# Rounding casts of the weight pieces queued behind the exponentials in a fused attention and feed-forward kernel

## Chip, cores, metric

The kernel runs on one core of one Trainium2 chip. The metric is the device time of one execution in microseconds; the time before is the median of three runs.

## What is computed

Block-causal attention (8 batches, 8 heads, 576 positions, 64 columns a head), whose output goes through two matrix products with a piecewise quadratic between them. Cut to what matters:

```python
scores = scale * np.matmul(q, k.transpose(0, 1, 3, 2))
scores = np.where(block_i >= block_j, scores, -1000000000.0)     # blocks of 64
attn = np.exp(scores - max) / (sum + 1e-09)
x = np.matmul(attn, v)                                           # -> 4608 x 512
h = x @ w_in                                                     # 512 x 2048
g = np.where(h >= 1, h, np.where(h <= -1, 0, (h + 1) ** 2 / 4))
out = g @ w_out                                                  # 2048 x 512
```

## The kernel before

TensorE multiplies in float32r, and float32 operands are split into a rounded part (hi) and the rest (lo). Three streams of work share the engines.

**Attention.** `attention_steps` goes through 32 pairs of heads (a batch and two neighbouring heads), eight steps a pair. A step traces one group of scores: `scores` (two products a tile on TensorE at L482 and L485, the row maximum on VectorE at L505, the exponential on ScalarE at L509, the inverse of the sum at L491 and L492, and the scaling of the probabilities `pr` on VectorE at L515), or `scores_last` (L529 to L541). Some steps later the probabilities are transposed (`turn`, L552 or L554), copied out of PSUM (L545) and multiplied with v (`weighted`, L591); the result is copied to `xh` and `xl` (L626, L627). The queries and keys of the next pair are prepared on the way: loads at L334 and L339, splits at L351 to L364, transposes at L422, copies at L427 and a copy by DMA at L433. The pairs of the first two batches are the eight that share their time with the weights. From the second batch on the probabilities are first moved by a DMA at L243.

**Weights.** `weight_pieces` cuts both matrices into 64 pieces of 128 x 256; `convert` splits one, in three stages that `prepare_weights` advances: (1) the load into `bits` (L164), two scalings on ScalarE (L169, L170), three operations on VectorE (L171, L174, L177); (2) an integer add on GpSimd (L183) and the rounding cast on ScalarE (L185) to `wih` or `ws`; (3) the subtract on GpSimd (L187), which leaves the lo part and lets the buffers go. The second piece of each pair of w_out pieces also stores the split rows to DRAM (L213). The feed-forward work reads them back (L787). `bits` and `work` have three buffers each, and odd pieces below 32 borrow the feed-forward buffers `t` and `gl`.

**Feed-forward.** `ffn_in` (L770 to L787) and `ffn_out` (L794 to L811) work on 512 tokens and 128 hidden columns a tile.

What sets the order: the main loop traces one step of attention, then the conversion stages that are due, then (from step 36) one half of a feed-forward tile. A scheduler then puts the traced instructions into one fixed order for each engine, and may take an instruction that is ready early ahead of others that were traced before it. At run time each engine and the SP queue, which issues all DMAs, take their instructions in that order, and wait with semaphores. So a cast at L185 may stand ahead of the exponentials of the step in which it was traced, or of earlier ones.

Of the kernel before, what the change touches and what calls it, by code (L numbers as in the profile page):

```python
# [23 lines left out]
def block_attn_then_ffn(  # L24
# [9 lines left out]
    nc = tc.nc  # L34
# [116 lines left out]
    for j in range(2):  # L151
        nc.sync.dma_start(qa[D:KA, j, :S].bitcast(F32), mrow[:, 0, :].bitcast(F32))
        nc.sync.dma_start(ka[D:KA, j, :].bitcast(F32), mrow[:, 1, :].bitcast(F32))


    def convert(n, source, hi, lo, done):

        if n < BORROW and n % 2:
            bits = ffn.tile([P, CW, 2], I32, tag="t", name="bits")
            work = ffn.tile([P, 2, CW], F32, tag="gl", name="work")  # L160
        else:
            bits = conv.tile([P, CW, 2], I32, tag="bits", name="bits")
            work = conv2.tile([P, 2, CW], F32, tag="work", name="work")
        nc.sync.dma_start(bits, source.bitcast(I32).rearrange("p (n t) -> p n t", t=2))  # L164
        top, mag = work[:, 0, :], work[:, 1, :].bitcast(U32)
        low = bits[:, :, 0]


        nc.scalar.mul(top, bits[:, :, 1].bitcast(F32), 2.0**-112)  # L169
        nc.scalar.mul(low, low.bitcast(U32), 2.0**-29)  # L170
        nc.vector.tensor_scalar(  # L171
            out=top, in0=top, scalar1=F32_TOP, scalar2=-F32_TOP, op0=ALU.min, op1=ALU.max
        )
        nc.vector.tensor_scalar(  # L174
            out=mag, in0=top.bitcast(U32), scalar1=3, scalar2=None, op0=ALU.logical_shift_left
        )
        nc.vector.scalar_tensor_tensor(  # L177
            out=mag, in0=top.bitcast(U32), scalar=0x80000000, in1=mag,
            op0=ALU.bitwise_and, op1=ALU.bitwise_or,
        )  # L180
        yield
        w32 = mag.bitcast(I32)
        nc.gpsimd.tensor_tensor(out=w32, in0=w32, in1=low, op=ALU.add)  # L183
        w32 = w32.bitcast(F32)
        nc.scalar.copy(hi(), w32)  # L185
        yield
        nc.gpsimd.tensor_tensor(out=lo(), in0=w32, in1=hi().bitcast(F32), op=ALU.subtract)  # L187
        if done:
            done()
# [65 lines left out]
    class Pair:  # L255
# [238 lines left out]
        def scores(self, j, g):  # L494
            tiles = self.GROUPS[g]
            m = len(tiles)
            ps = work_bank("ps_s")
            pr = att3.tile([P, S], F32, tag="pr", name="pr")
            nm = small.tile([P, 2], F32, tag="nm", name="nm")
            sm = small.tile([P, 2], F32, tag="sm", name="sm")  # L500
            cols = [slice(at, at + (t + 1) * P) for t, at in tiles]
            for (t, _), cs in zip(tiles, cols):
                self.product(ps[:, cs], j, t * P, 0, (t + 1) * P, True, True)
            for i, cs in enumerate(cols):
                nc.vector.tensor_reduce(  # L505
                    out=nm[:, i : i + 1], in_=ps[:, cs], axis=AX.X, op=ALU.max, negate=True
                )
            for i, cs in enumerate(cols):
                nc.scalar.activation(  # L509
                    pr[:, cs], ps[:, cs], AF.Exp, bias=nm[:, i : i + 1], scale=1.0,  # L510
                    accum_out=sm[:, i : i + 1],
                )
            self.inverse(sm[:, :m])
            for i, cs in enumerate(cols):
                nc.vector.tensor_scalar_mul(pr[:, cs], pr[:, cs], sm[:, i : i + 1])  # L515
            self.pr[j, g] = as_float32r(pr[:, : cols[-1].stop], self.plain) if self.hop else [pr]

        def scores_last(self):

            half = S // 2  # L520
            pr = att3.tile([P, S], F32, tag="pr", name="pr")
            nm = small.tile([P, 3], F32, tag="nm", name="nm")
            sm = small.tile([P, 3], F32, tag="sm", name="sm")
            banks = []
            for i in range(2):
                ps = work_bank("ps_s")
                for j in range(2):
                    self.product(ps[:, :half], j, SM, i * half, half, j == 0, j == 1)
                nc.vector.tensor_reduce(  # L529
                    out=nm[:, i : i + 1], in_=ps[:, :half], axis=AX.X, op=ALU.max, negate=True  # L530
                )
                banks.append(ps)
            nc.vector.tensor_tensor(out=nm[:, 2:3], in0=nm[:, 0:1], in1=nm[:, 1:2], op=ALU.min)
            for i in range(2):
                nc.scalar.activation(
                    pr[:, i * half : (i + 1) * half], banks[i][:, :half], AF.Exp,
                    bias=nm[:, 2:3], scale=1.0, accum_out=sm[:, i : i + 1],
                )
            nc.vector.tensor_tensor(out=sm[:, 2:3], in0=sm[:, 0:1], in1=sm[:, 1:2], op=ALU.add)
            self.inverse(sm[:, 2:3])  # L540
            nc.vector.tensor_scalar_mul(pr, pr, sm[:, 2:3])  # L541
            self.pr["last"] = as_float32r(pr, self.plain) if self.hop else [pr]
# [342 lines left out]
```

## Time and profile before

| | |
|---|---|
| median of 3 runs | 1266.43 us (1266.29 to 1266.98) |
| the profiled execution | 1269.69 us, of which 1267.9 us are the span that the profile shows |
| TensorE (PE) busy | 1200.1 us, 95% of the span |
| VectorE (DVE) busy | 887.0 us, 70% |
| ScalarE (ACT) busy | 703.2 us, 55% |
| GpSimd (POOL) busy | 394.6 us, 31% |
| casts at L185 | 64, at 13.5 to 253.1 us |

The span is the time from the first to the last instruction; the shares are averages over it, and the kernel has stages with different limits: the weights are converted only up to about 255 us. A row of a timeline gives the start, the duration, the engine, the line, what is written from what, and in brackets the idle time of the engine just before it and what ended that.

### The profile page before, as it was taken

The page shows a single profiled execution, that of the slowest core. Times are in us where ns is not written, and L with a number is a line of the kernel's source. Part 1 is how long each engine was busy: PE and PEld are TensorE (multiplying, and loading weights), DVE is VectorE, ACT ScalarE, POOL GpSimd, SP SyncE. Part 2 cuts the span into 40 slices and gives each one's busy share as a digit, 9 for nine tenths or more (in the row PEclk, how much of TensorE's full clock was granted, in tenths as well). Part 3 has the DMA queues.
Part 4 walks back from the last instruction along what each step waited for, and adds up shares of the span by engine and source line. Part 5 has one row for each costly group of instructions (what it writes and reads, how often), then busy time and mean ns, then how long its engine had stood idle before and what let it go on. Part 6 is the DMA issues. An engine that isn't in the chain of part 4 may idle for free.

```text
span 1267.9 us, 20253 instructions
## 1 busy us (share of the span) xinstructions
PE 1200.1 (95%) x6280; PEld 998.8 (79%) x6280; DVE 887.0 (70%) x2188; ACT 703.2 (55%) x1827; POOL 394.6 (31%) x430
## 2 busy tenths in 40 slices
PE   5888889899999999999999999999999999999998
PEld 4666667678888888888888888888888888888886
DVE  8898877758777777777777777787777777322222
ACT  5787656646566655665656655566556555222222
POOL 3555655522222222222222222222222222222222
PEclk9888988999999999999999999999999999999999
DMA  5566666667888655555554655465556433422432
GB/s 158 167 176 215 203 228 197 217 198 237 260 273 266 215 162 158 154 175 163 156 162 145 187 157 152 138 189 153 160 154 190 137 128 118 132 87 98 133 100 100
DMA packets 185259, 215.43 MB, mean 170 GB/s; under 512 B 113840, under 2 KB 132272, under 8 KB 184384
## 3 DMA queue, kind: packets, MB, share of 16 engines
q1 hardware_dynamic: 185152, 214.14, 54.9%
q8 instruction: 50, 0.82, 0.3%
q14 instruction: 57, 0.47, 0.1%
HBM read 134.74 MB, written 31.98 MB: 131 GB/s over the span
## 4 chain that ended last, share of the span: by engine, by line
PE 69%; DVE 16%; ACT 6%; issue 5%; DMA 1%; POOL 1%; SPq 1%; ACTq 0%; POOLq 0%; DVEq 0%
PE ph L770 29%; PE po L794 15%; PE po L799 7%; PE ps_av L591 7%; PE ps_s L482 4%; ACT pr L509 3%; PE ps_s L485 3%; DVE t L780 2%; PE ps_t L552 2%; DVE t L783 2%; ACT t L779 2%; DVE pb L547 2%; DVE nm L505 2%; DVE sm L491 1%; DVE pr L515 1%
## 5 line engine op out<-in xcount | busy, mean ns | idle before, releaser
L785 POOL TENSOR_TENSOR gl<-t,gh 128x512 fp32r<-128x512 f32 x144 | 187.5, 1302 | 510.2 <-ACT gh L784 333.2
L794 PE MATMUL po<-wo,gh 128*128 128x512 f32 x1152 | 296.1, 397 | 0.5 <-DMA wo<-wo_split 0.3
L794 PEld LDWEIGHTS po<-wo,gh 128*128 128x128 f32 x1152 | 212.5, 189 | 44.5 <-DMA wo<-wo_split 0.7
L770 PE MATMUL ph<-xh,wih 128*128 128x512 f32 x576 | 232.9, 404 | 1.6 <-DVE t L783 1.6
L770 PE MATMUL ph<-xh,wil 128*128 128x512 f32 x576 | 228.8, 397 | 0.0
L770 PE MATMUL ph<-xl,wih 128*128 128x512 f32 x576 | 227.8, 396 | 0.5 <-DVE xl L627 0.5
L780 DVE SCALAR_TENSOR_TENSOR t<-t 128x512 f32<-128x512 f32 x144 | 101.5, 705 | 168.0 <-ACT t L779 165.2
L779 ACT ACTIVATE t<-ph 128x512 f32<-128x512 f32 x144 | 85.9, 597 | 173.8 <-PE ph L770 173.8
L509 ACT ACTIVATE pr<-ps_s,nm 128x128 f32<-128x128 f32 (+3 forms) x256 | 134.1, 527 | 60.5 <-DVE nm L505 58.4
L784 ACT CAST gh<-t 128x512 fp32r<-128x512 f32 x144 | 89.5, 621 | 120.3 <-DVE t L783 120.0
L799 PE MATMUL po<-wo,gl 128*128 128x512 f32 x576 | 155.6, 392 | 0.0
L482 PE MATMUL ps_s<-ka,qa 68*128 68x288 f32 (+4 forms) x384 | 135.3, 367 | 15.0 <-ACT pr L509 5.4
L379 POOL TENSOR_TENSOR vsr<-vn,vsr 128x256 fp32r<-128x256 f32 (+1 forms) x96 | 55.2, 576 | 246.2 <-ACT vsr L378 244.6
L770 PEld LDWEIGHTS ph<-xh,wil 128*128 128x128 f32 x576 | 109.5, 190 | 23.8
L770 PEld LDWEIGHTS ph<-xh,wih 128*128 128x128 f32 x576 | 109.8, 191 | 21.7 <-DVE t L783 2.3
L799 PEld LDWEIGHTS po<-wo,gl 128*128 128x128 f32 x576 | 108.7, 189 | 23.1
L505 DVE TENSOR_REDUCE nm<-ps_s 128x1 f32<-128x128 f32 (+3 forms) x256 | 118.8, 482 | 10.4 <-PE ps_s L485 9.4
L770 PEld LDWEIGHTS ph<-xl,wih 128*128 128x128 f32 x576 | 109.7, 190 | 20.5 <-DVE xl L627 0.9
L485 PE MATMUL ps_s<-kb,qb 128*128 128x288 f32 (+4 forms) x384 | 121.1, 322 | 0.0
L515 DVE TENSOR_SCALAR pr<-pr,sm 128x128 f32<-128x128 f32 (+3 forms) x256 | 107.3, 440 | 5.4
L783 DVE TENSOR_TENSOR t<-ph,t 128x512 f32<-128x512 f32 x144 | 98.7, 686 | 2.2
L491 DVE TENSOR_SCALAR sm<-sm 128x1 f32<-128x1 f32 (+1 forms) x224 | 52.0, 232 | 68.3 <-ACT pr L509 65.7
(111 smaller groups left out, 1871.4 us busy)
## 6 DMA issues: line engine op xcount, KB each, us to landing
wo<-wo_split SPq DMA_DIRECT2D x144, 512.0 KB, 3.5
prr<-pr SPq DMA_DIRECT2D x96, 192.0 KB, 2.5
prr<-pr SPq DMA_DIRECT2D x72, 256.0 KB, 2.8
out_dram<-ob SPq DMA_DIRECT2D x36, 256.0 KB, 2.9
bits<-in_moe_w_in_dram SPq DMA_DIRECT2D x32, 256.0 KB, 3.5
bits<-in_moe_w_out_dram SPq DMA_DIRECT2D x32, 256.0 KB, 3.0
wo_split<-ws SPq DMA_DIRECT2D x16, 512.0 KB, 2.9
qa<-qb SPq DMA_DIRECT2D x63, 128.0 KB, 2.4
```

What stands on the lines that cost most here:

```text
L482: nc.tensor.matmul(ps, qa[:KA, j, c0 : c0 + P], ka[:KA, j, k0 : k0 + n], start=first, stop=False)
L485: nc.tensor.matmul(ps, qb[:, j, c0 : c0 + P], kb[:, j, k0 : k0 + n], start=False, stop=last)
L505: nc.vector.tensor_reduce(out=nm[:, i : i + 1], in_=ps[:, cs], axis=AX.X, op=ALU.max, negate=True)
L509: nc.scalar.activation(pr[:, cs], ps[:, cs], AF.Exp, bias=nm[:, i : i + 1], scale=1.0, accum_out=sm[:, i : i + 1],)
L515: nc.vector.tensor_scalar_mul(pr[:, cs], pr[:, cs], sm[:, i : i + 1])
L770: nc.tensor.matmul(ph, w[:, cc, fs], x[:, cc, xs], start=(cc == 0 and i == 0), stop=(cc == NCC - 1 and i == 2),)
L779: nc.scalar.activation(t_, ph, AF.Relu, bias=0.5, scale=0.5)
L780: nc.vector.scalar_tensor_tensor(out=t_, in0=t_, scalar=1.0, in1=t_, op0=ALU.min, op1=ALU.mult)
L783: nc.vector.tensor_tensor(out=t_, in0=ph, in1=t_, op=ALU.max)
L785: nc.gpsimd.tensor_tensor(out=gl, in0=t_, in1=gh.bitcast(F32), op=ALU.subtract)
L794: nc.tensor.matmul(po[tt], gh[:, ts_], wo[:, w, :], start=(fc == 0 and w == 0), stop=False)
L799: nc.tensor.matmul(po[tt], gl[:, ts_], wo[:, 0, :], start=False, stop=fc == NFC - 1)
```

## The change

The exponentials are collected in a list as they are traced, and the rounding cast gets an ordering edge to the latest of them: on ScalarE it is issued behind that exponential. The edge sets the order in the queue and adds no wait of its own. No instruction is added or removed.

```diff
+    exps = []
+
...
         w32 = w32.bitcast(F32)
-        nc.scalar.copy(hi(), w32)
+
+        with tc.issue_after(exps[-1].ins):
+            nc.scalar.copy(hi(), w32)
         yield
...
             for i, cs in enumerate(cols):
-                nc.scalar.activation(
+                exps.append(nc.scalar.activation(
                     pr[:, cs], ps[:, cs], AF.Exp, bias=nm[:, i : i + 1], scale=1.0,
                     accum_out=sm[:, i : i + 1],
-                )
+                ))
...
             for i in range(2):
-                nc.scalar.activation(
+                exps.append(nc.scalar.activation(
                     pr[:, i * half : (i + 1) * half], banks[i][:, :half], AF.Exp,
                     bias=nm[:, 2:3], scale=1.0, accum_out=sm[:, i : i + 1],
-                )
+                ))
```

In the rows of order below the lines of the changed kernel stand two higher inside `convert` ahead of the cast (L171 is L173, L174 is L176, L177 is L179, L164 is L166) and four higher from the cast on (L185 is L189, L491 is L495, L505 is L509, L509 is L513, L515 is L519, L213 is L217, L433 is L437).

ScalarE, the first pair: the first cast and the exponentials of the first step, before.

```order
L169 ACTIVATE work<-bits 128x256
L185 CAST wih<-work 128x256
L456 CAST kb<-ps_qk 128x2x64
L170 ACTIVATE bits<-bits 128x256
L509 ACTIVATE pr,sm<-ps_s,nm 128x128
L509 ACTIVATE pr,sm<-ps_s,nm 128x256
L509 ACTIVATE pr,sm<-ps_s,nm 128x384
```

The same place now.

```order
L171 ACTIVATE work<-bits 128x256
L172 ACTIVATE bits<-bits 128x256
L460 CAST kb<-ps_qk 128x2x64
L513 ACTIVATE pr,sm<-ps_s,nm 128x128
L513 ACTIVATE pr,sm<-ps_s,nm 128x256
L189 CAST wih<-work 128x256
L513 ACTIVATE pr,sm<-ps_s,nm 128x384
```

The cast went behind two exponentials. Of the 64 casts 30 have more exponentials ahead of them than before, 29 as many and 5 fewer, since the scheduler places everything anew.

VectorE, the second half of the fourth pair, from the scaling of the last rows' probabilities on, before (twelve consecutive rows).

```order
L515 TENSOR_SCALAR pr<-pr,sm 128x256
L491 TENSOR_SCALAR sm<-sm 128x1
L177 SCALAR_TENSOR_TENSOR work<-work 128x256
L492 RECIPROCAL sm<-sm 128x1
L174 TENSOR_SCALAR work<-work 128x256
L515 TENSOR_SCALAR pr<-pr,sm 128x384
L505 TENSOR_REDUCE nm<-ps_s 128x1
L177 SCALAR_TENSOR_TENSOR work<-work 128x256
L171 TENSOR_SCALAR work<-work 128x256
L174 TENSOR_SCALAR work<-work 128x256
L177 SCALAR_TENSOR_TENSOR work<-work 128x256
L491 TENSOR_SCALAR sm<-sm 128x1
```

The same place now.

```order
L519 TENSOR_SCALAR pr<-pr,sm 128x256
L495 TENSOR_SCALAR sm<-sm 128x1
L496 RECIPROCAL sm<-sm 128x1
L519 TENSOR_SCALAR pr<-pr,sm 128x384
L509 TENSOR_REDUCE nm<-ps_s 128x1
L495 TENSOR_SCALAR sm<-sm 128x1
L496 RECIPROCAL sm<-sm 128x1
L519 TENSOR_SCALAR pr<-pr,sm 128x512
L631 TENSOR_TENSOR xl<-ps_av,xh 128x256
```

Six conversion operations have left this place: a later cast lets its buffers go later, so the next pieces are loaded and converted later. Two pieces more than before stand in the second half of the fifth pair, where the counts are equal again.

The SP queue at the end of the fourth pair, before.

```order
L164 DMA bits<-in_moe_w_out_dram 128x512
L433 DMA ka<-kb 64x512
L213 DMA wo_split<-ws 128x1024
L164 DMA bits<-in_moe_w_out_dram 128x512
L433 DMA qa<-qb 64x512
L433 DMA ka<-kb 64x512
```

The same place now.

```order
L217 DMA wo_split<-ws 128x1024
L437 DMA qa<-qb 64x512
L166 DMA bits<-in_moe_w_out_dram 128x512 x2
L437 DMA ka<-kb 64x512
L166 DMA bits<-in_moe_w_out_dram 128x512
L217 DMA wo_split<-ws 128x1024
L437 DMA qa<-qb 64x512
```

The stores of the split weights went back in the queue and now stand directly ahead of copies that attention needs. Of the 16 stores 4 had such a copy (L433 or L243) directly behind them before, and 10 have one now.

## Rows read from the trace of the kernel before

**Rows 1.** The page: its span and the engines' busy times.

```profile
span 1267.9 us, 20253 instructions
PE 1200.1 (95%) x6280; PEld 998.8 (79%) x6280; DVE 887.0 (70%) x2188; ACT 703.2 (55%) x1827; POOL 394.6 (31%) x430
```

**Rows 2.** Busy by stretch: length, PE, PEld, DVE, ACT, POOL, granted clock, DMA share, GB/s.

```profile
88.00:100.00 12.00, 7.82 (x58) 6.28 (x57) 11.86 (x38) 10.78 (x33) 7.59 (x10) 1.00 0.66 198
100.00:108.00 8.00, 8.00 (x30) 5.59 (x31) 6.64 (x24) 4.97 (x17) 4.19 (x6) 0.79 0.51 178
260.00:1267.90 1007.90, 988.00 (x5244) 831.54 (x5244) 674.60 (x1608) 530.59 (x1327) 258.94 (x259) 1.00 0.53 164
```

**Rows 3.** The casts at L185, and what they wait for: total us, times.

```profile
L185 ACT CAST wih<-work x32: 394/406/422, 13.5 to 240.3; 128x256 fp32r<-128x256 f32 x32
...
  POOL work L183: 30.6, 31
```

**Rows 4.** TensorE's timeline, the idle times at the end of the fourth pair.

```profile
90.51 0.66 PE L554 MATMUL ps_t<-ident_r,pr 128*128 128x128 f32 x4 [0.72 <-DVE pr L515]
92.98 0.74 PE L554 MATMUL ps_t<-ident_r,pr 128*128 128x128 f32 x5 [1.46 <-ACT pr L509]
95.84 0.55 PE L554 MATMUL ps_t<-ident_r,pr 128*128 128x128 f32 x3 [0.53 <-DVE pr L515]
99.92 0.63 PE L554 MATMUL ps_t<-ident_r,pr 128*128 128x128 f32 x4 [1.47 <-DVE pr L515]
```

**Rows 5.** VectorE in 90.6 to 98.9 us, of L171, L174 and L177 alone, in turn.

```profile
90.60:98.90 8.30, 1.36 (x3) 1.00 0.76 231
...
90.60:98.90 8.30, 1.55 (x4) 1.00 0.76 231
...
90.60:98.90 8.30, 1.65 (x4) 1.00 0.76 231
```

**Rows 6.** VectorE's timeline: conversions of the fourth pair, idle times of the fifth.

```profile
90.98 0.28 DVE L171 TENSOR_SCALAR work<-work 128x256 f32<-128x256 f32 x1
...
94.71 0.27 DVE L174 TENSOR_SCALAR work<-work 128x256 uint32<-128x256 uint32 x1
...
96.31 0.41 DVE L177 SCALAR_TENSOR_TENSOR work<-work 128x256 uint32<-128x256 uint32 x1
96.64 0.81 DVE L171 TENSOR_SCALAR work<-work 128x256 f32<-128x256 f32 x1
...
122.11 0.69 DVE L505 TENSOR_REDUCE nm<-ps_s 128x1 f32<-128x512 f32 x1 [0.47 <-PE ps_s L485]
123.65 0.15 DVE L491 TENSOR_SCALAR sm<-sm 128x1 f32<-128x1 f32 x1 [0.84 <-ACT pr L509]
```

**Rows 7.** GpSimd's timeline around 97 us.

```profile
95.53 1.77 POOL L187 TENSOR_TENSOR ws<-work,ws 128x256 fp32r<-128x256 f32 x2
```

**Rows 8.** Timelines at the second pair's end: VectorE's last scaling, TensorE's transposes of it.

```profile
55.67 0.92 DVE L515 TENSOR_SCALAR pr<-pr,sm 128x512 f32<-128x512 f32 x1
...
57.88 0.60 PE L554 MATMUL ps_t<-ident_r,pr 128*128 128x128 f32 x4
```

**Rows 9.** The longest idle time on TensorE after 100 us, and ScalarE's queue ahead of it.

```profile
226.19 0.44 PE L482 MATMUL ps_s<-ka,qa 68*128 68x384 f32 x1 [3.66 <-ACT kb L427]
...
224.76 0.40 ACT L185 CAST ws<-work 128x256 fp32r<-128x256 f32 x1 [1.98 <-POOL work L183]
225.07 0.59 ACT L779 ACTIVATE t<-ph 128x512 f32<-128x512 f32 x1
225.56 0.58 ACT L427 CAST kb<-ps_qk 128x512 fp32r<-128x512 f32 x1
```

**Rows 10.** TensorE's timeline: eight equal products, twice.

```profile
100.86 3.86 PE L591 MATMUL ps_av<-pb,vs 128*128 128x320 f32 x8
105.01 2.21 PE L591 MATMUL ps_av<-pb,vs 128*128 128x320 f32 x8
```

**Rows 11.** Waits of the SP queue up to 260 us: total us, times, longest.

```profile
SPq L213 <- POOL ws L187: 16.6, 11, 3.6
```

## Prediction

> **What bounds the kernel now.** I read the page first, then busy time by stretch, then the waits of the line that the change moves, and last the timelines of the engines it touches. The page [rows 1] gives TensorE 1200.1 us of a span of 1267.9, so TensorE is idle for 67.8 us; no other engine comes near. The stretches [rows 2] say where: from 260 us on TensorE is busy for 988.0 of 1007.9 us, idle 19.9, so 47.9 us of idle time lie ahead of 260 us, where the weights are converted and all 64 casts run. The work on TensorE is the same in both orders, and after 260 us it stands in the same order. So whatever TensorE loses or gains ahead of 260 us shifts all the rest by as much, and only that counts.
>
> The casts themselves [rows 3] take some 0.4 us each. What they cost beside that is ScalarE's waiting for the integer add on GpSimd: 30.6 us, 31 times. Behind a waiting cast stand exponentials and copies that TensorE wants; the change puts the newest exponential ahead of the cast. Its second effect is on VectorE: a later cast gives its buffers back later, so later pieces are converted later. At the end of the fourth pair this falls on a full engine: from 88 to 100 us VectorE is busy for 11.86 of 12 us [rows 2], while TensorE has four idle times, 0.72, 1.46, 0.53 and 1.47 us [rows 4], three of them released by scaled probabilities (L515) and one by an exponential.
>
> **The change, part by part.** The sum is made against the median, 1266.43 us. The durations are those of one execution of 1269.69 us, 3.26 above that median; since each term is a difference, it carries over. About 0.2% (2.5 us) is what a measurement of this kernel can tell from no change.
>
> *Instructions.* None is added or removed, and the edge is one of order, so no semaphore is waited for anew: 0.
>
> *End of the fourth pair.* Between 90.6 and 98.9 us VectorE runs eleven conversion operations for 1.36 + 1.55 + 1.65 = 4.56 us [rows 5]. Four of them now go from ahead of the scaling of 384 columns (0.28 + 0.27 + 0.28 + 0.41 = 1.24 by their kinds [rows 6]), one L177 of 0.41 comes in earlier, so 0.83 us less stand there; and the four between that scaling and the one of 512 columns all leave (the seven ahead take about 2.2 by the short rows, which leaves these 2.36 of the 4.56 us). That is more than the idle times of 0.53 and of 1.47 us that these scalings release [rows 4], so both go: -2.0 us. The first two keep about what they have, since one follows an exponential and the operations ahead of the other only change places. Ends: 0, if the exponential is late next, and -4.2, if all four go.
>
> *The fifth pair.* The pieces come back. By the two orders, at VectorE's 33rd row maximum (L505) 23 pieces have been begun where 25 were; at the 41st both orders have 34, the two having caught up in the second half of the fifth pair. A piece costs VectorE 0.28 + 0.27 + 0.41 = 0.96 us by the short rows [rows 6], two cost 1.92. VectorE's idle time there is 0.47 + 0.84 = 1.31 us [rows 6], which hides as much: +0.6 us. Ends: 0 and, with no cover, +1.9. A page of the Trainium skill speaks against this price: SBUF — State Buffer, section Who interferes with whom, says that VectorE's scalar operations in their two-port modes and GpSimd lock each other out, whichever began first keeping the port for its whole length. The trace agrees, in one L171 of 0.81 us in place of 0.28 [rows 6] while GpSimd ran two subtracts from 95.53 us on [rows 7]. By that rule two pieces at the rate of the crowded stretch (4.56 / 11 x 6 = 2.5 us) would give +1.2 in place of +0.6, and a sum of 1264.3.
>
> *The second pair.* One piece stands a little earlier on VectorE, ahead of the last scaling. That scaling ends at 55.67 + 0.92 = 56.59 us and TensorE takes its transposes at 57.88 without idling [rows 8]: 1.29 us of cover for 0.96 us. 0; uncovered it would be +1.0.
>
> *ScalarE, 130 to 260 us.* Many casts still stand only two or three us behind their own scaling, so most of the waiting stays. The largest place is at 226.19 us, where TensorE idles for 3.66 us for a copy of keys (L427) at 225.56 us, which stands behind a cast that waited 1.98 us and an L779 of 0.59 [rows 9]. There the L779 now goes ahead of the cast and falls into its wait, so the copy is 225.56 - 225.07 = 0.49 us earlier: -0.5. Ends: -3.7, if the copy comes free of the casts altogether, and +1.0, if one mean wait (30.6 / 31 [rows 3]) lands on a copy that is in time now.
>
> *The clock.* TensorE's granted clock is 0.79 from 100 to 108 us [rows 2], behind the idle times of rows 4: for part of that stretch it runs at the lower level, 1.2 of 2.4 GHz. Eight products take 3.86 us at 100.86 and the same eight 2.21 us at 105.01 [rows 10], 1.65 us apart. With half of the idle time gone I take half of it: -0.8. Ends 0 and -1.7.
>
> Sum: -2.0 + 0.6 - 0.5 - 0.8 = -2.7, that is **1263.7 us**. With the favourable ends of ScalarE and of the clock (-2.0 - 3.7 - 1.7, and the fifth pair at 0) it is -7.4, 1259.0.
>
> **Rivals.** *Given back.* The two pieces find no cover in the fifth pair (+1.9 in place of +0.6), and new idle times there pull the clock down again (0 in place of -0.8): -2.0 + 1.9 - 0.5 = -0.6, 1265.8 us, no measurable change. For it: the conversions are drawn out where GpSimd works beside them [rows 6, 7]. Against it: VectorE has idle time in the fifth pair [rows 6], in the crowded stretch almost none [rows 2].
>
> *It does not do what it says.* The edge points to the exponential traced last, and 34 of 64 casts have no more exponentials ahead than before. If the buffers' return, not the order, sets when the pieces come, the two pieces are only late by name and ScalarE waits as before: 1266.4 us.
>
> *Slower: the SP queue.* The stores of split weights (L213) now stand directly ahead of ten copies that attention needs (L433, L243), against four, because a later cast gives a later subtract. A store that waits for its subtract holds all loads and copies behind it. Such waits are 16.6 us in 11 times, 1.5 on the mean, 3.6 at most [rows 11]. If two of the six added ones reach TensorE, each costs 1.5 and, as the clock falls behind an idle time, up to 1.65: +6.3, and with -2.7 the time is 1266.43 + 3.6 = 1270.0 us. The point from which it decides: a store's subtract ends later than the copy's own source is ready. For it: the subtract comes last in a piece. Against it: the stores stand later themselves, when their subtract may be long done, and copies of keys and queries are issued steps ahead of the product that reads them.
>
> **How the numbers follow.** The forecast has 0.42: the fourth pair's end is the one place where the difference of order and the idle times meet in the trace, and its size is near the limit of what can be told. Given back has 0.28, the change without effect 0.08, the SP queue 0.22. From these: faster 0.42, same 0.28 + 0.08 = 0.36, slower 0.22. The range is 1259.0 to 1270.0: the favourable ends below, the SP rival's price above, with about one in ten outside at either side. The forecast's own range is 1259.0 to 1263.9, the upper end being the limit of what can be told; what falls above that counts as given back.
>
> **What would show it.** Right: in the profile after, the idle times of 0.53 and 1.47 us behind L515 are gone from the end of the fourth pair, VectorE is less than full there, the products of 100.86 us all take about 2.2 us, and the waiting of the casts for GpSimd is some us below 30.6; TensorE's idle time ahead of 260 us falls by about 2 from 47.9. Given back shows as new idle times released by L505 or L515 between 108 and 135 us. The SP rival shows as a larger wait of L213 for GpSimd, with TensorE waiting for products that read keys or queries copied by L433. The forecast is wrong if the last exponential of the fourth pair, not the scaling, releases TensorE there, or if TensorE's idle time grows at places where neither order differs by a row that I named.

## Result, and the profile after

The changed kernel takes 1272.87 us (median of four runs, 1271.83 to 1274.93), the kernel before 1266.70. The ratio measured over the runs is 1.0036, interval 1.0018 to 1.0053; the two medians by themselves are 1.0049 apart. All ratios below are measured like the first, against runs of before on the same chip. Six more runs on another chip gave 1.0039 (1.0026 to 1.0051). The change makes the kernel slower by about 5 us, where 2.7 us less had been forecast; the time lies above the range.

The page after answers to [rows 1]:

```profile
span 1270.1 us, 20248 instructions
PE 1195.8 (94%) x6280; PEld 996.7 (78%) x6280; DVE 888.9 (70%) x2188; ACT 704.2 (55%) x1827; POOL 394.2 (31%) x430
```

The profiled execution took 1271.83 us, the lowest of the four, and that of before was 3.26 above its median, so that the two traces are only 2.2 us apart; what follows goes by stretches. Busy time of the stretches of [rows 2], and of the one between them that those rows leave out, after:

```profile
88.00:100.00 12.00, 9.21 (x54) 7.99 (x53) 9.51 (x32) 9.59 (x30) 5.55 (x7) 0.72 0.46 137
100.00:108.00 8.00, 7.20 (x35) 5.20 (x33) 7.49 (x23) 5.46 (x19) 3.00 (x5) 1.00 0.76 230
108.00:130.00 22.00, 15.97 (x73) 12.70 (x74) 15.79 (x41) 13.36 (x37) 10.98 (x13) 0.69 0.60 192
260.00:1270.10 1010.10, 988.70 (x5254) 832.25 (x5253) 676.02 (x1610) 532.37 (x1328) 258.73 (x257) 1.00 0.53 163
```

From 108 to 130 us the kernel before had:

```profile
108.00:130.00 22.00, 19.34 (x111) 15.99 (x109) 18.80 (x47) 15.40 (x44) 10.48 (x14) 0.92 0.64 196
```

VectorE is no longer full from 88 to 100 us (9.51 of 12 us, before 11.86), as forecast. But ahead of 260 us TensorE now idles for 260 - (1195.8 - 988.7) = 52.9 us, before 47.9; and the stretch in which it lost most is the one from 108 to 130 us, where it is busy for 15.97 us with 73 products at a granted clock of 0.69, before for 19.34 us with 111 at 0.92.

Each order was traced a second time: the changed kernel as f1 and the orders of before as g3, both below. In f1 TensorE idles for 52.2 us ahead of 260 us, in g3 for 48.2, so that this difference holds. From 108 to 130 us g3 had:

```profile
108.00:130.00 22.00, 17.12 (x104) 14.20 (x105) 19.33 (x50) 16.28 (x46) 12.31 (x16) 1.00 0.64 208
```

The pairs of heads show where the time went. Each starts with a score product of 128 columns (L482, now L486); the table has the time from start to start, from TensorE's timelines of two executions of each order (g3 and f1 are the second ones).

| us | pairs 1 to 3 | pair 4 | pair 5 | pair 6 | from pair 7 to the end |
|---|---|---|---|---|---|
| before | 66.8 | 18.6 | 30.3 | 44.5 | 1095.3 |
| before, second execution | 65.9 | 21.8 | 28.9 | 42.8 | 1096.0 |
| changed | 63.8 | 22.1 | 34.0 | 43.9 | 1093.9 |
| changed, second execution | 63.0 | 23.5 | 33.8 | 44.0 | 1092.8 |

On the means the change gains 3.0 us in the first three pairs, which had not been forecast, loses 2.6 in the fourth, 4.3 in the fifth and 0.3 in the sixth, and gains 2.3 later. That is 2.0 us in all, of a loss of about 5: the two executions of before that were traced took 1269.69 and 1269.42 us, longer than the median of their runs (1266.70 and 1267.65), so the pairs show where the orders differ, but not the whole loss.

**The fourth pair.** TensorE's idle times there, after, and the eight products of [rows 10]:

```profile
86.46 0.33 PE L486 MATMUL ps_s<-ka,qa 68*128 68x128 f32 x1 [1.30 <-DVE xl L631]
...
89.45 1.12 PE L558 MATMUL ps_t<-ident_r,pr 128*128 128x128 f32 x4 [1.19 <-DVE pr L519]
...
92.80 1.30 PE L558 MATMUL ps_t<-ident_r,pr 128*128 128x128 f32 x5 [1.60 <-DVE sm L495]
...
98.81 0.60 PE L558 MATMUL ps_t<-ident_r,pr 128*128 128x128 f32 x4
...
99.72 2.17 PE L595 MATMUL ps_av<-pb,vs 128*128 128x320 f32 x8
```

Of the four idle times of [rows 4] the last two, 0.53 and 1.47 us, are gone, and the eight products take 2.17 us in place of 3.86. But the first two have grown (1.19 and 1.60, before 0.72 and 1.46), one of 1.30 us is there that [rows 4] do not have, and the lower clock has only moved: 0.72 from 88 to 100 us, where it was 1.00, and 1.00 from 100 to 108 us, where it was 0.79.

That can't be put down to the change, for g3, which has the orders of before, shows nearly the same:

```profile
88.99 0.54 PE L429 MATMUL ps_qk<-ident_r,qs 128*128 128x128 f32 x4 [1.45 <-DVE xl L634]
...
91.20 1.12 PE L561 MATMUL ps_t<-ident_r,pr 128*128 128x128 f32 x4 [0.91 <-DVE pr L522]
...
94.13 1.30 PE L561 MATMUL ps_t<-ident_r,pr 128*128 128x128 f32 x5 [1.17 <-DVE sm L498]
...
101.40 2.17 PE L598 MATMUL ps_av<-pb,vs 128*128 128x320 f32 x8
```

Idle times like those of 0.53 and 1.47 us are missing there, although the four conversions still stand between the two scalings, and its fourth pair takes 21.8 us. Its granted clock, too, is 0.72 from 88 to 100 us and 1.00 from 100 to 108. Only VectorE's room is the change's own: in g3 VectorE is busy for 11.29 of the 12 us, nearly as before. In e2 and f4, whose orders there are also those of before, both idle times are present (0.51 and 1.35, 0.52 and 1.44) and the pair takes 18.7 and 18.6 us. So one order has two courses here.

**The fifth pair.** TensorE's timeline after:

```profile
109.19 0.42 PE L556 MATMUL ps_t<-ident_r,vsr 128*128 128x128 f32 x3 [1.95 <-DMA vsr<-pr]
...
111.28 0.63 PE L774 MATMUL ph<-xh,wil 128*128 128x512 f32 x1
113.52 0.72 PE L556 MATMUL ps_t<-ident_r,prs 128*128 128x128 f32 x4 [1.61 <-ACT t L783]
...
118.23 0.79 PE L774 MATMUL ph<-xh,wih 128*128 128x512 f32 x1 [3.23 <-DVE t L787]
```

The three idle times are 6.79 us together, and the pair has no others (6.53 in f1). Before, the whole pair had 3.56 us (5.01 in g3): the 1.47 us of [rows 4], and these two, of which the second answers to the 3.23 (1.65 in g3):

```profile
112.47 0.45 PE L552 MATMUL ps_t<-ident_r,vsr 128*128 128x128 f32 x3 [1.41 <-DMA vsr<-pr]
113.61 0.50 PE L770 MATMUL ph<-xh,wih 128*128 128x512 f32 x1 [0.68 <-DVE t L783]
```

L774 (before L770) is the first product of a feed-forward tile. The products of a tile go to the one PSUM buffer of ph, so the second tile waits until the first has been read for the last time, by the maximum at L787 (before L783). VectorE's conversions and evacuation between the first tile's products and that maximum, after:

```profile
112.24 0.28 DVE L173 TENSOR_SCALAR work<-work 128x256 f32<-128x256 f32 x1
112.50 0.75 DVE L173 TENSOR_SCALAR work<-work 128x256 f32<-128x256 f32 x1
113.24 0.74 DVE L176 TENSOR_SCALAR work<-work 128x256 uint32<-128x256 uint32 x1
114.34 0.41 DVE L179 SCALAR_TENSOR_TENSOR work<-work 128x256 uint32<-128x256 uint32 x1
114.74 0.28 DVE L176 TENSOR_SCALAR work<-work 128x256 uint32<-128x256 uint32 x1
115.06 0.83 DVE L179 SCALAR_TENSOR_TENSOR work<-work 128x256 uint32<-128x256 uint32 x1
...
116.77 0.68 DVE L784 SCALAR_TENSOR_TENSOR t<-t 128x512 f32<-128x512 f32 x1
117.49 0.69 DVE L787 TENSOR_TENSOR t<-ph,t 128x512 f32<-128x512 f32 x1
```

The first tile's last product ends at 111.28 + 0.63 = 111.91 us, its maximum at 118.18: 6.27 us. In between stand two whole pieces, six operations of 3.29 us, with a scaling of probabilities between and behind them. Before, the products ended at 109.49 us and the maximum came by 113.55:

```profile
109.45 0.42 DVE L177 SCALAR_TENSOR_TENSOR work<-work 128x256 uint32<-128x256 uint32 x1
110.21 1.03 DVE L780 SCALAR_TENSOR_TENSOR t<-t 128x512 f32<-128x512 f32 x1 [0.35 <-issue]
...
112.87 0.68 DVE L783 TENSOR_TENSOR t<-ph,t 128x512 f32<-128x512 f32 x1
```

That is 4.06 us, with a single conversion operation of 0.42 us at its start. So here the postponed pieces have come back: in the second half of the pair, as the orders had shown, but ahead of a maximum that TensorE waits for, and not at VectorE's idle times of 122.11 and 123.65 us [rows 6]. The two other idle times of 1.95 and 1.61 us stand ahead of transposes of probabilities that a DMA brings (in f1 the second is 1.35 and put down to that DMA).

**ScalarE and the SP queue.** The waits of the cast, after:

```profile
  POOL work L185: 30.2, 26
```

and of the stores:

```profile
SPq L217 <- POOL ws L191: 15.5, 13, 2.6
```

The casts wait as long as before (30.6 us in [rows 3]), and the stores a little less (16.6 in [rows 11]). The longest wait of [rows 9] is 1.14 us shorter, but behind a new one of 1.86 us:

```profile
225.86 0.72 PE L556 MATMUL ps_t<-ident_r,prs 128*128 128x128 f32 x4 [1.86 <-DMA prs<-pr]
229.10 0.69 PE L486 MATMUL ps_s<-ka,qa 68*128 68x384 f32 x1 [2.52 <-ACT kb L431]
```

### The profile page after: what moved, and what is told of

Its sections match the earlier page's. It is cut to its first block, busy times and chain, and to the rows that moved or that the text cites. A ratio compares the mean times of both kernels' runs of the same rounds, so it can differ in the third digit from the quotient of the medians.

```text
span 1270.1 us, 20248 instructions
## 1 busy us (share of the span) xinstructions
PE 1195.8 (94%) x6280; PEld 996.7 (78%) x6280; DVE 888.9 (70%) x2188; ACT 704.2 (55%) x1827; POOL 394.2 (31%) x430
## 4 chain that ended last, share of the span: by engine, by line
PE 63%; DVE 7%; ACT 4%; issue 2%; ACTq 0%
PE ph L774 26%; PE po L798 15%; PE po L803 7%; PE ps_av L595 5%; PE ps_s L486 4%; PE ps_s L489 2%; ACT pr L513 2%; PE ps_t L556 2%; DVE t L784 1%; DVE pb L551 1%; DVE t L787 1%; ACT t L783 1%; DVE sm L495 1%; PE ps_qk L405 1%; DVE x L618 1%
## 5 line engine op out<-in xcount | busy, mean ns | idle before, releaser
L774 PE MATMUL ph<-xh,wih 128*128 128x512 f32 x576 | 232.5, 404 | 4.0 <-DVE t L787 4.0
L774 PE MATMUL ph<-xh,wil 128*128 128x512 f32 x576 | 227.7, 395 | 0.0
L774 PE MATMUL ph<-xl,wih 128*128 128x512 f32 x576 | 226.9, 394 | 0.0
L784 DVE SCALAR_TENSOR_TENSOR t<-t 128x512 f32<-128x512 f32 x144 | 101.0, 702 | 160.4 <-ACT t L783 157.6
L783 ACT ACTIVATE t<-ph 128x512 f32<-128x512 f32 x144 | 85.9, 597 | 164.5 <-PE ph L774 164.5
L513 ACT ACTIVATE pr<-ps_s,nm 128x128 f32<-128x128 f32 (+3 forms) x256 | 134.4, 529 | 67.7 <-DVE nm L509 65.9
L486 PE MATMUL ps_s<-ka,qa 68*128 68x288 f32 (+4 forms) x384 | 136.0, 369 | 14.0 <-ACT pr L513 6.0
L383 POOL TENSOR_TENSOR vsr<-vn,vsr 64x64 fp32r<-64x64 f32 (+1 forms) x96 | 55.4, 578 | 242.6 <-ACT vsr L382 240.8
L774 PEld LDWEIGHTS ph<-xh,wih 128*128 128x128 f32 x576 | 109.4, 190 | 24.0 <-DVE t L787 5.2
L774 PEld LDWEIGHTS ph<-xh,wil 128*128 128x128 f32 x576 | 109.3, 190 | 23.9
L774 PEld LDWEIGHTS ph<-xl,wih 128*128 128x128 f32 x576 | 109.5, 190 | 19.2
L509 DVE TENSOR_REDUCE nm<-ps_s 128x1 f32<-128x128 f32 (+3 forms) x256 | 119.0, 482 | 7.5 <-PE ps_s L489 6.6
L519 DVE TENSOR_SCALAR pr<-pr,sm 128x128 f32<-128x128 f32 (+3 forms) x256 | 105.4, 433 | 5.7 <-DVE sm L496 0.3
L495 DVE TENSOR_SCALAR sm<-sm 128x1 f32<-128x1 f32 (+1 forms) x224 | 55.4, 247 | 70.5 <-ACT pr L513 67.9
L787 DVE TENSOR_TENSOR t<-ph,t 128x512 f32<-128x512 f32 x144 | 98.7, 686 | 2.3
```

The source lines that it names most:

```text
L486: nc.tensor.matmul(ps, qa[:KA, j, c0 : c0 + P], ka[:KA, j, k0 : k0 + n], start=first, stop=False)
L509: nc.vector.tensor_reduce(out=nm[:, i : i + 1], in_=ps[:, cs], axis=AX.X, op=ALU.max, negate=True)
L513: exps.append(nc.scalar.activation(pr[:, cs], ps[:, cs], AF.Exp, bias=nm[:, i : i + 1], scale=1.0, accum_out=sm[:, i : i + 1],))
L774: nc.tensor.matmul(ph, w[:, cc, fs], x[:, cc, xs], start=(cc == 0 and i == 0), stop=(cc == NCC - 1 and i == 2),)
L783: nc.scalar.activation(t_, ph, AF.Relu, bias=0.5, scale=0.5)
L784: nc.vector.scalar_tensor_tensor(out=t_, in0=t_, scalar=1.0, in1=t_, op0=ALU.min, op1=ALU.mult)
```

## Experiments

Pieces are counted from 0. Most kernels give the edge to some pieces alone, by one condition:

```diff
-        with tc.issue_after(exps[-1].ins):
-            nc.scalar.copy(hi(), w32)
+        if CONDITION:
+            with tc.issue_after(exps[-1].ins):
+                nc.scalar.copy(hi(), w32)
+        else:
+            nc.scalar.copy(hi(), w32)
```

### Parts of the change, and two remedies

**e1**, `n < 16`:

> The edge for the first 16 pieces alone; the orders of the first three pairs change as in the changed kernel, and from the fourth pair on they are nearly those of before (first feed-forward evacuation on ScalarE behind 43 exponentials, as before; 48 in the changed kernel). Theory (the loss arises in the fifth pair, where the first feed-forward tile is evacuated late): the gain of the first pairs, 2.7 to 3.2 us at 57 to 80 us in the changed kernel's trace, stays: 1263.5 us, at most 1265. Rival (the loss arises all along, in the waits of later stages, and eats any lead): 1266 to 1268.

Measured 1.0016 (1.0004 to 1.0029), 1268.95 us, against the theory: the lead was there and was lost. Its trace is of the slowest of its twelve runs, 1275.51 us. Pairs 1 to 3 take 62.8 us in it, 3 to 4 us less than before, but the fourth and fifth, with their orders of before, 23.1 and 31.2 us. They run at a lower clock than before (0.91 and 0.92 in these stretches, 0.83 and 1.00 in g3):

```profile
88.00:108.00 20.00, 16.50 (x80) 13.22 (x79) 17.81 (x56) 13.67 (x43) 11.19 (x15) 0.76 0.58 182
108.00:130.00 22.00, 20.02 (x99) 16.59 (x99) 16.95 (x45) 15.19 (x43) 10.22 (x12) 0.78 0.59 186
```

Over its twelve runs the mean granted clock is 0.9794, in the 29 runs of before on that chip 0.9815. What that is worth can be estimated from runs of one program: straight lines through the runs of before on each of the five chips, and through those of e2 below, give 0.34 to 0.83 us for each 0.001 of the mean clock. So the 0.0021 are 0.7 to 1.7 us, a part of the lead; where the rest was lost is not shown.

**e2**, `n >= 24`:

> The edge from piece 24 on alone; the first four pairs as before, the first evacuation behind 43 exponentials, later casts placed as in the changed kernel, 6 stores ahead of copies (10 in the changed kernel, 4 before). Theory (fifth pair alone): within 2 us of before, 1265 to 1269. Rival (late casts or the SP queue slow the stretch from 130 to 260 us): 1270 or more.

1.0025 (1.0012 to 1.0039), 1271.26 us: above the theory's bounds, within the rival's. The fifth pair is as before (31.0 us in its trace), but the trace is of one of its faster runs, 1266.44 us, and can't show what the slower ones lost.

**e3**, piece 25 in buffers of its own:

```diff
-        if n < BORROW and n % 2:
+        if n < BORROW and n % 2 and n != 25:
```

> The changed kernel, but piece 25 does not borrow the feed-forward buffers t and gl and takes those of its own pools. The first feed-forward tile then takes a buffer that came free a piece earlier; its evacuation on ScalarE stands behind 43 exponentials again, with three fewer conversion operations ahead of it on VectorE (81, not 84). Theory A (a borrowed buffer that comes free late holds back the first evacuation, and TensorE waits 3.2 us for it at the lower clock): the wait at 118 us goes and the time falls to 1263 to 1267. Theory B (only the two pieces' operations on VectorE hold it back): at most a third of the loss returns, 1270 or more.

1.0051 (1.0037 to 1.0065), slower than the changed kernel. The count had misled: the evacuation begins on ScalarE at once, but five conversion operations (2.30 us) still stand ahead of the maximum, and TensorE's wait is as long:

```profile
115.19 0.79 PE L774 MATMUL ph<-xh,wih 128*128 128x512 f32 x1 [3.06 <-DVE t L787]
```

**e4**, pieces 26 to 28 behind the first maximum (`evac` holds the instructions of L787; a plain context where there is none yet):

```diff
+        with tc.issue_after(evac[0].ins) if n in (26, 27, 28) and evac else loose:
             nc.vector.tensor_scalar(
...
         want += LAG
+        if i == START:
+            want = 26
```

> The changed kernel, but pieces 26 to 28 are ordered on VectorE behind the first feed-forward tile's maximum (piece 26 is issued one step later for it): 78 conversion operations ahead of that maximum, not 84; on ScalarE the first evacuation stays behind 48 exponentials. Theory B (the postponed pieces on VectorE hold back the first evacuation): two pieces, about 2.3 us, and the lower clock behind them go, 1264 to 1268. Theory A (the buffer and ScalarE's order hold it back): at most 1.5 us return, 1271 or more.

1.0026 (1.0015 to 1.0037), 1270.0 us, between the two theories. The wait for the maximum falls from 3.23 to 0.51 us, but the transposes ahead of it now wait for longer, 2.63 in place of 1.61:

```profile
112.92 0.72 PE L559 MATMUL ps_t<-ident_r,prs 128*128 128x128 f32 x4 [2.63 <-DMA prs<-pr]
...
114.92 0.80 PE L777 MATMUL ph<-xh,wih 128*128 128x512 f32 x1 [0.51 <-DVE t L790]
```

### The late evacuation alone, and the middle pieces

**f1**, the changed kernel again:

> The changed kernel once more, on the chip of the next three. Every theory: 1.0036 of before as measured, 1.0018 to 1.0053.

1.0039 (1.0026 to 1.0051). Its trace shows the same 3.23 us in the fifth pair.

**f2**, the kernel before with one edge, on the first tile's evacuation:

```diff
-        nc.scalar.activation(t_, ph, AF.Relu, bias=0.5, scale=0.5)
+        with tc.issue_after(exps[-1].ins) if (c, fc) == (0, 0) else __import__("contextlib").nullcontext():
+            nc.scalar.activation(t_, ph, AF.Relu, bias=0.5, scale=0.5)
```

> The kernel before with one edge alone: the first feed-forward tile's evacuation on ScalarE (L779) behind the newest exponential. No cast has an edge, and the orders of the first four pairs are those of before; in the fifth that evacuation stands behind 48 exponentials, and 84 conversion operations ahead of its maximum on VectorE, as in the changed kernel (before 43 and 82). Theory (the loss is the late first evacuation): slower by 3 to 6 us, 1.0024 to 1.0047 of before, with an idle time of about 3 us on TensorE released by that maximum. Rival (the loss is spread over the later casts and stores): within 1.5 us of before.

1.0028 (1.0015 to 1.0040), within the theory's range. The idle time is there, with another name: the transposes of prs, which wait for a DMA, and no feed-forward product can fill the gap, since the maximum ends only at 117.83 us.

```profile
116.54 0.72 PE L559 MATMUL ps_t<-ident_r,prs 128*128 128x128 f32 x4 [4.13 <-DMA prs<-pr]
117.88 0.79 PE L777 MATMUL ph<-xh,wih 128*128 128x512 f32 x1
```

Pairs 4 and 5 take 52.9 us together in this trace (before 48.9 and 50.7). But the fifth by itself takes 31.1 us (30.3 and 28.9), 1.5 more on the mean, with 4.98 us of idle time, which is no more than in g3 (5.01). The sixth takes 49.8 (44.5 and 42.8), and the rest 1089.6 (1095.3 and 1096.0). On its page TensorE idles for 1271.3 - 1200.3 = 71.0 us, before for 67.8 and in g3 for 67.7, and is busy for as long as there. So the late evacuation goes with a loss, and in this trace the loss is idle time; that it arises in the fifth pair is not shown. The mean clock of its runs is lower by 0.0021 (0.9790, of before 0.9811), by the estimate above 0.7 to 1.7 us of the 3.4 us between the mean times, 1271.16 and 1267.74.

**f3**, `16 <= n < 24`:

> The edge for pieces 16 to 23 alone, those of the third and fourth pair that are late in the fifth: the first evacuation behind 46 exponentials, 87 conversion operations ahead of its maximum. Theory (the fifth pair): slower by 3 to 6 us, 1.0024 to 1.0047. Rival (the first 16 and the pieces from 24 on, measured at 1.0016 and 1.0025, make up the whole loss together): 0.999 to 1.001.

1.0002 (0.9989 to 1.0015): against the theory, the rival's number, though the wait for the first maximum was 3.75 us in its trace. Pairs 4 and 5 take 51.7 us together (before 48.9 and 50.7), and from pair 7 on it has 4 us less than before. A wait of this size in the fifth pair need not cost anything in the whole.

**f4**, `n < 8`:

> The edge for the first 8 pieces alone: the orders differ from before in the first two pairs only. Theory (an early exponential is worth what the trace of the changed kernel shows there, 2.5 to 3 us at 57 us, and nothing later eats it where the order is that of before): faster by 1.5 to 3 us, 0.9976 to 0.9988. Rival (a lead of the first pairs is lost to the lower clock or to later waits): 0.9995 to 1.002.

1.0005 (0.9993 to 1.0018), against the theory. It is the rival's number, but not for its reason, as no lead was there to lose: pairs 1 to 3 take 66.8 us. By these traces the gain of the first pairs comes with pieces 8 to 15.

### Pieces 16 to 23, one side and the other

**g1**, `not 16 <= n < 24`:

> The changed kernel without the edge for pieces 16 to 23: in the first two pairs and from piece 24 on the casts stand as in the changed kernel, in the fourth and fifth nearly as before (first evacuation behind 43 exponentials, 83 conversion operations ahead of its maximum). Theory (the fifth pair makes most of the loss): TensorE's wait for that maximum at about 113 to 118 us is 1 us or less and the ratio falls from 1.0039 to at most 1.0015. Rival (the loss is that of the two other parts, 1.0016 and 1.0025 by themselves): 1.003 to 1.005.

1.0012 (0.9996 to 1.0029), within the theory's bound; on a second chip (i2) 1.0011 (1.0001 to 1.0020). The first tile's maximum ends 4.0 us after its products again, but TensorE's wait for it is 1.97 us, where the theory had 1 us or less, and the fifth pair still takes 32.8 us (33.1 in i2). So without the edges of 16 to 23 most of the changed kernel's loss is gone, but its fifth pair (33.9 us on the mean) is only about 1 us longer than here.

**g2**, `16 <= n < 20`:

> The edge for pieces 16 to 19 alone: first evacuation behind 43 exponentials, 80 conversion operations ahead of its maximum. Theory: the wait in the fifth pair stays at 1 us or less, and by it nothing is lost there: 0.998 to 1.001 with what other orders do later. Rival (any new order of the conversions costs, wherever it falls): 1.0015 to 1.004.

1.0034 (1.0019 to 1.0050), against the theory as it was put. But the trace shows the wait, 3.44 us: three conversions stand between the products and the maximum, although fewer conversions stand ahead of it in all. The count of what stands ahead in all was the wrong measure. The three take only 0.99 us, though; the 5.24 us between have other long operations of VectorE too, such as the feed-forward tile's own first one (L787, 1.19 us; in the changed kernel it is L784 and takes 0.68, before L780 with 1.03).

**g3**, the condition `n < 0`:

> The kernel before under the changed source, no piece with an edge: the same orders on every engine. Every theory: 1.000; its distance from 1.000 is what two sets of runs of one program differ by, and its profile shows a second execution of the orders of before.

1.0001 (0.9989 to 1.0012).

**g4**, e3 and e4 together:

> The changed kernel with both of the earlier remedies: piece 25 does not borrow the feed-forward buffers, and pieces 26 to 28 are behind the first maximum on VectorE. First evacuation behind 43 exponentials, 78 conversion operations ahead of its maximum. Theory (that evacuation held back on both engines): the wait of 3.2 us for it goes to under 1 us, and the ratio from 1.0039 to at most 1.002. Rival (the loss is spread over the later stages): 1.003 or more.

1.0055 (1.0038 to 1.0072), the rival's side. Two conversions of 0.72 us together still stand between, the tile's own first operation on VectorE (L787) takes 1.85 us, 5.5 us pass from the products to the maximum, and the wait is the longest of all for it:

```profile
114.06 0.79 PE L777 MATMUL ph<-xh,wih 128*128 128x512 f32 x1 [3.99 <-DVE t L790]
```

### A measure that sorts most of them

The time from the end of the first tile's products to the end of its maximum, read from each trace as above:

| kernel | products to maximum, us | wait of the next tile, us | ratio |
|---|---|---|---|
| before; g3 | 4.06; 4.06 | 0.68; 1.65 | 1; 1.0001 |
| f4 first 8 | 4.06 | 1.01 | 1.0005 |
| g1 without 16 to 23 | 4.02 | 1.97 | 1.0012 |
| e1 first 16 | 4.07 | 1.00 | 1.0016 |
| e2 from 24 | 3.88 | 0.85 | 1.0025 |
| f3 pieces 16 to 23 | 4.54 | 3.75 | 1.0002 |
| e4 pieces behind | 4.57 | 0.51, and 2.63 on prs | 1.0026 |
| f2 late evacuation | 7.92 | 0, and 4.13 on prs | 1.0028 |
| g2 pieces 16 to 19 | 5.24 | 3.44 | 1.0034 |
| changed; f1 | 6.27; 6.01 | 3.23; 3.23 | 1.0036; 1.0039 |
| g4 both remedies | 5.51 | 3.99 | 1.0055 |
| e3 own buffer | 6.34 | 3.06 | 1.0051 |

Above 1.0020 all but e2 have 4.5 us or more; with as much, f3 alone stayed low, and its 4.54 us are as good as e4's 4.57, with 1.0026 there. The ratios do not add up by pieces either: pieces 16 to 19 alone cost 0.0034, and with 20 to 23 nothing. The next runs asked whether that time is the cause.

**h1**, no edge, and the feed-forward half steps traced one step earlier:

```diff
-        if i >= START:
+        if i >= 35:
             banks["free"] = False
```

> The kernel before, no edge, the feed-forward half steps traced from step 35 on, not 36. On VectorE 7 operations stand between the last xl of the first 512 tokens and the first maximum (before 11, changed kernel 27), and none is a scaling of probabilities. Theory (the time from the first tile's products to its maximum is the cause): it falls from 4.1 us to 2 to 3 us, TensorE's wait for that maximum goes, and the time is 0.9980 to 0.9995 of before. Rival (it only goes along with other orders): 1.0000 to 1.003.

1.0013 (0.9997 to 1.0028): the rival. The time fell to 2.84 us, yet TensorE waits 2.08 us for the maximum all the same, as it now arrives there earlier:

```profile
110.69 0.50 PE L777 MATMUL ph<-xh,wih 128*128 128x512 f32 x1 [2.08 <-DVE t L790]
```

So a shorter time than that of before gave nothing here. The mean clock of these runs is higher than that of before (0.9853, before 0.9818), and that gave nothing either.

**h2**, the same with `not 16 <= n < 24`:

> The edge for all pieces but 16 to 23, and the feed-forward half steps from step 35 on: 7 operations there too. Theory: the lead of 3 us at 86 us is not lost in the fifth pair, 0.9970 to 0.9995. Rival: at least as slow as the same without the earlier half steps, 1.0012 or more.

1.0005 (0.9995 to 1.0016): neither. It is no worse than g1, and the lead does not reach the end, at a mean clock of 0.9851.

**h3**, `not 18 <= n < 24`:

> The changed kernel without the edge for pieces 18 to 23 alone: 11 operations between the last xl and the first maximum, as before. Theory: 4.0 to 4.1 us from the products to the maximum, and at most 1.0015 of before. Rival: 1.003 or more, near the changed kernel's 1.0039.

0.9951 (0.9933 to 0.9970), faster than both kernels. That is within the theory's bound, but it named no gain. The maximum comes 4.00 us after the products, and the wait is short:

```profile
110.36 0.80 PE L777 MATMUL ph<-xh,wih 128*128 128x512 f32 x1 [0.93 <-DVE t L790]
```

### Is it the two pieces 16 and 17?

**i1**, h3 again:

> The changed kernel without the edge for pieces 18 to 23, again, on another chip. Theory (its order gives more of the higher clock: 0.987 on the mean of its runs, where before had 0.982): 0.993 to 0.997 again. Rival (a lucky set of runs): 0.999 to 1.002.

0.9949 (0.9934 to 0.9963), 1259.98 us where before had 1267.46. The maximum comes 4.00 us after the products again, yet TensorE waits 2.24 us for it, longer than before (0.68, and 1.65 in g3): the gain does not lie in this wait. The page:

```profile
PE 1192.1 (95%) x6280; PEld 995.2 (79%) x6280; DVE 886.6 (70%) x2188; ACT 703.2 (56%) x1827; POOL 395.4 (31%) x430
```

Of the span of 1258.2 us TensorE idles for 66.1 (66.7 in h3), before for 67.8, in g3 for 67.7. So the gain is for the most part shorter busy time of the same 6280 products: 1192.1 us, in h3 1193.2, against 1200.1 and in g3 1199.9.

**i2**, g1 again:

> The changed kernel without the edge for pieces 16 to 23, again, on the chip of i1. If the order makes the difference: 1.000 to 1.003, apart from i1 by more than both intervals; if the chip does: like i1.

1.0011 (1.0001 to 1.0020): the order makes the difference, not the chip. TensorE's page has 1198.4 us busy and 68.9 idle.

**i3**, `n < 18`:

> The edge for the first 18 pieces alone; the first 16 alone gave 1.0016. If the casts of pieces 16 and 17 give the gain by themselves: 0.993 to 0.998. If it takes the later pieces (from 24 on) with them: 0.9995 to 1.002.

0.9988 (0.9979 to 0.9997): between the two. Against e1, on another chip, 0.0028 come with pieces 16 and 17, and the rest up to i1 with the edges of 24 and later, which alone (e2) cost 0.0025. The mean granted clock of the runs goes along: 0.9872 in i1, 0.9831 in i3, 0.9815 in i2, 0.9826 in the 21 runs of before on that chip. By the estimate given with e1 the 0.0046 between i1 and before are worth 1.6 to 3.8 us of the 6.5 us between their mean times, 1266.95 and 1260.49. And a higher mean clock is not enough: h1 and h2 had 0.9853 and 0.9851, and on their pages TensorE is busy for 1203.1 and 1202.0 us, longer than before.

## Why the prediction was wrong

**The bound** was right in the main: TensorE's idle time ahead of 260 us grew by 4.5 us on the mean of two executions each. But it did not stay at the same 19.9 us behind 260 us, as assumed; there it is 21.4 and 22.8 us in the changed kernel, 19.9 and 19.5 before.

**The end of the fourth pair**, "-2.0 us", was not had. The four conversions left, VectorE got room, and the idle times of 0.53 and 1.47 us are not in the changed kernel's traces. But they are not in g3 either, where the conversions stand as before, so it is not shown that the conversions made them: the term was read from one execution, and another of the same order lacks its idle times. And "the first two keep about what they have" was wrong: they grew by 0.61 us together, and one of 1.30 us came with them (in g3 1.45). The pair takes 22.1 and 23.5 us in the changed kernel, 18.6 and 21.8 before: +2.6 us on the mean, less than the two executions of before are apart.

**The fifth pair is the step that failed** most plainly, "+0.6 us", with +1.9 as its worst end. It measured 34.0 and 33.8 us against 30.3 and 28.9, so +4.3 on the mean: 2.4 of these are TensorE's idle time (6.79 and 6.53 us, before 3.56 and 5.01), and the rest goes with the lower clock from 108 to 130 us (0.69 in both executions, before 0.92 and 1.00). Three things were wrong in it. The cover: the two orders were known to be level again at the 41st row maximum, with the two pieces in the second half of the fifth pair, and VectorE's idle times of 0.47 and 0.84 us there were set against them; but those stand behind the place where the pieces came back, which is ahead of the first feed-forward maximum. The price: an operation there does not cost its own duration against VectorE's idle time, since TensorE's next tile waits for that maximum and has no second buffer; that wait is 3.23 us in both executions, before 0.68 and 1.65. How much of the 4.3 us it costs by itself is not shown: g1 and i2, with 4.0 us from products to maximum, still take 32.8 and 33.1 us, e4 has the wait at 0.51 us and 1.0026, and f3 has 3.75 us of it and 1.0002. And the durations: the six operations took 3.29 us (2.82 in f1), not 1.92, three of them 0.74 to 0.83 us in place of 0.27 to 0.41. Beside two of the three GpSimd was at its subtracts:

```profile
112.26 1.58 POOL L191 TENSOR_TENSOR wil<-work,wih 128x256 fp32r<-128x256 f32 x2
```

So the rule of the Trainium skill (SBUF — State Buffer, Who interferes with whom), which the prediction weighed and left out of its sum, agrees with this trace: L173 took 0.75 us and L176 0.74 beside that work. The two came out 0.75 + 0.74 - 2 x 0.28 = 0.93 us longer than the short rows. By the rule alone the fifth pair's term would still have been +1.2 us, not +4.3: what the pieces were set against was the larger error.

**ScalarE.** The casts' waits did not shrink (30.2 us, before 30.6). At 226 us the wait became 2.52 in place of 3.66 us, as a smaller number had been forecast, but 1.86 us arose just ahead of it.

**The clock.** The forecast gave back 0.8 us, in the products of 100.86 us. They do take 2.17 us, but so they do in g3, and the lower clock lies elsewhere: the granted clock is 0.83 from 88 to 108 us (before 0.91, in g3 0.83) and 0.69 from 108 to 130 (0.92 and 1.00). Over the whole execution it is the same as before (0.981 on the mean of the runs). On the pages TensorE idles for 74.3 us (75.0 in f1), before for 67.8 (67.7 in g3), and is busy for 1195.8 (1194.3), before for 1200.1 (1199.9): the loss is TensorE's idle time, and a part of it is given back as shorter busy time.

**The rivals.** The SP queue, the rival on the slower side, did not come about: its stores waited 15.5 us, at most 2.6. *Given back* was the nearest, but the sign for it named L505 and L515 as the releasers, and it was L783 (now L787), with DMAs of probabilities beside it. Not seen at all was the gain of 3 us in the first three pairs.

**What stays open.** The edge loses 5 us when all pieces have it, and gains 6 us when pieces 18 to 23 have none (h3, i1). Of these 11 us the traces place the following, on the mean of two executions each: 0.8 us in pairs 1 to 3 (63.4 and 62.7 us), 2.4 in pair 4 (22.8 and 20.4), 2.8 in pair 5 (33.9 and 31.1), 4.0 in pair 6 (43.9 and 39.9) and 0.5 after that. So the late evacuation in the fifth pair is a part of the cost, at most these 2.8 us here, and by g1 and i2 (32.8 and 33.1 us without it) rather 1. Why the order of the changed kernel loses 5 us in the whole stays open. So does why pieces 16 and 17 are worth 7.9 us beside the later ones (1259.98 us in i1, 1267.92 in i2), with the same time from products to maximum. The pages of h3 and i1 differ from those of g1 and i2 both in TensorE's idle time (66.7 and 66.1 us against 71.6 and 68.9) and in its busy time (1193.2 and 1192.1 against 1196.7 and 1198.4). The mean clock of the runs goes along with that (0.9873 and 0.9872 against 0.9808 and 0.9815), but h1 and h2 show that a higher one is not by itself a gain; what in the order makes the difference was not tested.

## What to carry to other kernels

A scheduler that places everything anew turns a small ordering edge into a new order some steps away, so count what the new order puts between a producer and the consumer that frees a buffer without a spare, here the one PSUM buffer of a feed-forward tile; work that is postponed does not go where an engine idles, but where its turn comes. Before a sum is built on idle times of half a microsecond or one and a half, trace the same order a second time: here two of the four were gone without any change. A gain in early stages is worth its price only if what follows does not give it back, which an experiment on the early part alone (e1) can show. And try an edge on parts of a loop: here all of it costs 5 us, and without six of 64 pieces it gains 6, which the theory of that run (h3) did not name.

## What the runs showed of the hardware

The same orders get the lower clock in different places from one execution to the next. Those of before took 18.6 us for the fourth pair in one execution and 21.8 us in another (g3), with granted clocks of 0.91 and 0.83 from 88 to 108 us. The twelve runs of e2, one program on one chip, show what that is worth: four took 1265.53 to 1267.58 us at mean clocks of 0.985 and 0.986, seven 1271.18 to 1273.16 us at 0.978 to 0.980, with one between. Differences of a few us between two single traces of this kernel prove little, which is why the pairs above are read from two executions where there are two.
